# Logits and half-tile rows turned by VectorE and ScalarE instead of TensorE, with two loads and one sum moved

## The chip, the cores and the metric

The kernel runs on one core of a Trainium2 chip. The metric is the device time of one launch in microseconds (us). A profile of one execution comes with the times; in it PE is TensorE (PEld its weight loads), DVE is VectorE, ACT is ScalarE, POOL is GpSimd and SP is SyncE, and L12 is line 12 of the kernel.

## The reference

Linear attention with decay over 4 sequences of 768 tokens and 8 heads of 64, and on its output (3072 rows of 512) a mixture of 8 experts with a sticky choice of expert:

```python
for b in range(nb):                       # blocks of the sequence
    intra = einsum('bhic,bhjc->bhij', qb, kb) * Dmask
    intra = einsum('bhij,bhjd->bhid', intra, vb)
    inter = einsum('bhid,bhde->bhie', qb * lam_pow, kv_state)
    out[:, :, sl] = intra + inter
    kv_state = lam_block * kv_state + einsum('bhsd,bhse->bhde', kb_dec, vb)
...
logits = x @ w_gate;  local_gate = sigmoid(x @ w_local)
for s in range(S):                        # along each sequence
    e = argmax(logits[b, s]) if s == 0 or local_gate[b, s] < 0.5 else prev_e
    p = softmax(logits[b, s])
    out[b, s] = p[e] * (relu(x[b, s] @ w1[e]) @ w2[e])
```

w1 is 8 x 512 x 1024 and w2 is 8 x 1024 x 512. All is in fp32.

## The kernel before

**Attention half** (lines 785 to 842). 24 steps s, one for each block of 128 tokens of each of the 4 sequences, blocks outermost. A step multiplies queries and keys of a later step (`scores`, L196 to L212: on TensorE, then VectorE's product with the decay mask into `sm`), adds the state's part (`from_state`, L235) and the block's part (`mix`, L248), which ScalarE copies to `xc` (L251), brings the state up to date (`update`, L262 to L267), and turns the rows of the step before and writes them to a DRAM buffer (`rows_of`, L272 to L281). `WIDE` lists the steps whose scores are made with 128 keys in one matmul (L200); the others use two matmuls of 64 keys, the second of which leaves out queries that the mask makes zero (L208).

After every fourth step, `gates(k)` (L286) multiplies four finished blocks by the gate's weights. The 512 features lie in four groups of 128, and group d's partial logits come out on partitions 32d to 32d+8 of the bank `pl`, tokens along the free axis. ScalarE copies them to `lg` (L289). `logits(k)`, in the next step but for the last group, turns `lg` by four transposes on TensorE (L294), and VectorE adds the four partial sums of each token into `lt` (L295), which has tokens on partitions. From `lt` VectorE finds experts (`fresh_experts`, L399 to L403, its last output being `mark`), TensorE and VectorE follow them along the sequences (L411 to L420), rank the tokens, and build lists of rows for tiles of 128 tokens that share an expert. This routing is spread over the steps by the table `extras` (L771).

In this half the orders of PE, DVE, SP and POOL are those of the program text (L785). ScalarE's order is left to the scheduler of the framework, up to L916.

**First tiles** (L871 to L916). Five tiles of 128 rows go through `hidden` (L731, relu in L733) and `output` (L737), weights for each from `weights` on SP's queue. The rows are gathered by POOL's indirect DMA (L703). `flipped` (L717) turns 32x32 blocks of a gathered tile on VectorE, and `moved` (L724) brings the blocks to their places by 16 copies of 32 partitions, as a rule on ScalarE; `ks` names which quarters of the tokens it moves.

**Pairs** (L975 to L1077, from L1180 on with the orders of PE, DVE, SP and ACT by hand). Two tiles of one expert are multiplied together by a scheme with seven products for eight (`product_1` L957, `product_2` L962), which needs sums of blocks of the weights (`sums_1`, `sums_2`, L935 to L938) and of the rows (`sums_of_x`), all on VectorE. The last sum of `sums_2`, index 3, writes `s2[:, 2]`, read by the last but one product of the pair (L1064). While a pair runs, the next pair's two tiles are flipped and moved (L989, L990, L996, L1042 to L1059). Eight pairs run in the profiled execution, with three full tiles between the third and the fourth.

**Half tiles** of up to 64 rows are worked off in the first two pairs: `hook(0)` to `hook(13)` are places in a pair's program, and `hooks_of_halves` (L1128) puts a half's four steps on successive places. With three halves, as here, the first begins at hook 7 of pair 0, the second at hook 0 of pair 1 and the third at hook 7 of pair 1. The first has at most 32 rows. `turned_part` (L1083) turns the gathered rows `xgh` by four transposes on TensorE (L1086) and one copy on VectorE (L1088); `hidden_of_part` (L1096), `hidden_turned` (L1106) and `output_of_part` (L1118) follow. The halves' weights use a third pair of buffers, `w1t[2]` and `w2t[2]`.

**SP's queue** around the start of the pairs: the first layer of the first pair (L911), both layers of the first half (`weights_of(G2, 2)`, L914), then the second layer of the first pair (L1182). Each is 2 MB, and each waits until its buffer has been read for the last time: the first pair's second layer until `output(1, 1)` is done.

Of the kernel before, what the change touches and what calls it, by code (L numbers as in the profile page):

```python
# [38 lines left out]
PARTS = [(0, 8), (8, NA), (NA, NT)]  # L39
LOADS = 6  # L40
QUARTERS = [16, 17, 18, 19]
WIDE = [3, 4, 5, 6]
WARM = 10
KA = -(-(NA * P - E * (P - 1)) // P)

# [19 lines left out]
def kernel(  # L65
# [217 lines left out]
    def gates(k):  # L283

        for d in range(DT):
            nc.tensor.matmul(pl[EP * d:EP * d + EP], lhsT=wgt[:, d], rhs=xc[:, d].rearrange("p b i -> p (b i)"),  # L286
                             start=True, stop=True, skip_group_check=True)
        lg = lgs[k] = rt.tile([P, B * P], F32, name="lg")
        nc.scalar.copy(lg, pl)  # L289

    def logits(k):
        lg = lgs.pop(k)
        for j in range(B):
            nc.tensor.transpose(pl[:, P * j:P * j + P], lg[:, P * j:P * j + P], ident)  # L294
        nc.vector.tensor_reduce(lt[:, B * k:B * k + B],  # L295
                                pl.rearrange("p (j d e) -> p j e d", j=B, e=EP)[:, :, :E + 1],
                                axis=AX.X, op=ALU.add)

    pl = pg.tile([P, B * P], F32, name="pl")
    pr = pg.tile([P, DM], F32, name="pr")  # L300
# [381 lines left out]
    def weights_of(g, i, layers=(1, 2), cond=None, own=None):  # L682
        e = expert(g, own)
        if 1 in layers:
            nc.sync.dma_start(out=w1t[i], in_=w1_src(e), cond=cond, cond_hint=None if cond is None else True)
        if 2 in layers:
            nc.sync.dma_start(out=w2t[i], in_=w2_src(e), cond=cond, cond_hint=None if cond is None else True)
# [31 lines left out]
    def moved(xt, xq, ks=range(4), copy=nc.scalar.copy):  # L719

        blocks = xq.rearrange("p (d j i) -> p d j i", j=4, i=QP)
        for k in ks:
            for j in range(4):
                copy(xt[QP * j:QP * j + QP, :, QP * k:QP * k + QP], blocks[QP * k:QP * k + QP, :, j])  # L724
# [60 lines left out]
    with tc.manual_schedule(engines={PE, DVE, SP, POOL}):  # L785
# [16 lines left out]
        for s in range(NS):  # L802
            if s + LOADS - 1 < NS:
                loaded(s + LOADS - 1)
            if s + 3 < NS and s != 1:
                prepare(s + 3)
            if s in QUARTERS:
                j = QUARTERS.index(s)
                nc.sync.dma_start(out=w1t[0][:, j], in_=w1_src(0)[:, j])
            if s == NS - 4:  # L810
                nc.sync.dma_start(out=w2t[0], in_=w2_src(0))
                weights(0)
            if s == NS - 1:
                nc.sync.dma_start(out=w1t[1], in_=w1_src(1))
                nc.sync.dma_start(out=w2t[1], in_=w2_src(1))
            if s + 1 < NS and s not in (1, 2, 3, 4, 5):
                scores(s + 1)
            from_state(s)
            if s % B == 1 and s > B:
                logits(s // B - 1)  # L820
            if s == 5:
                scores(6)
            extra_work(s, 0)
            if s % B == 0 and s:
                gates(s // B - 1)
            mix(s)
            if s == 0:
                update(0)
                query_powers(0)
            if s in (1, 2, 3, 4):  # L830
                scores(s + 1)
            if s == 1:
                query_powers(1)
                prepare(4)
                rows_of(0)
            if s:
                update(s)
            if s + 1 == NS:
                first_turned()
            if s > 1:  # L840
                rows_of(s - 1)
            extra_work(s, 1)
# [38 lines left out]
        moved(xtt[1], xq, (2, 3))  # L881
        hidden(0, 0, 1)
        by_slots(0, (2, 3, 4))
        logits(NC - 1)
        fresh_experts(2)
        flipped(xqs[1], xgt[0])
        ahead(4, 0)
# [23 lines left out]
        weights_of(KA, w_of(0), (1,))  # L911
        output(1, 1, range(FT // 2))
        by_slots(1, (0, 1, 2, 3, 4))
        weights_of(G2, 2)  # L914
        output(1, 1, range(FT // 2, FT))
        written(3, 1)  # L916

# [4 lines left out]
    def xp(p, j):  # L922
        return xps[2] if j else xps[p % 2]
# [21 lines left out]
    def sums_2(p, ns):  # L945
        fs = sums(s2, b2(p, 0, 0), b2(p, 0, 1), b2(p, 1, 0), b2(p, 1, 1), False)
        for n in ns:
            fs[n]()
# [5 lines left out]
    def product_1(to, a, b, new=False):  # L954
        for m in range(FT // 2):
            for k in range(2):
                nc.tensor.matmul(to[:, m], lhsT=a[:, k, P * m:P * m + P], rhs=b[:, k], start=(new and not m and not k),  # L957
                                 stop=(k == 1), skip_group_check=True)
# [13 lines left out]
    def pair_moved(p, i):  # L972
        moved(xp(p, i), xqs[i])

    def pair(p, hooks={}, next=True, load=True, cond=None, write=True, further=True):  # L975

        def hook(k):
            for f in hooks.get(k, ()):
                f()
# [7 lines left out]
        nc.scalar.copy(c01, a)  # L987
        if next:
            pair_flipped(0)  # L989
            pair_moved(p + 1, 0)  # L990
        hook(0)
        product_1(b, s1[:, 1], xs[:, 1], True)
        tt(c10, c01, b, ALU.add)
        hook(1)
        sums_2(p, (0, 1))
        if next:  # L996
            pair_flipped(1)
# [6 lines left out]
        tt(c11, c11, c, ALU.add)  # L1004
        nc.scalar.activation(h11, c11, ACT.Relu)
        hook(3)
        sums_2(p, (2, 3))
        product_1(a, a1(p, 0, 1), b1(p, 1, 0))
        nc.scalar.activation(h00, a, ACT.Relu)
        hook(4)  # L1010
# [46 lines left out]
        hook(10)  # L1057
        if next:
            moved(xp(p + 1, 1), xqs[1], (3,))  # L1059
            sums_1(p + 1, (2, 3))  # L1060
        product_2(a, h01, b2(p, 1, 0))
        gated(c00, a, g1)
# [17 lines left out]
    def ahead_half(h):  # L1080
        collect(xgh, 1, G2 - KA + h)

    def turned_part(n):  # L1083
        pt = pg.tile([P, DT, P], F32, name="po1")
        for d in range(DT):
            nc.tensor.transpose(pt[:, d], xgh[:, P * d:P * d + P], ident)  # L1086
        xt = act.tile([P, DT, HP], F32, name="xth", bufs=1)[:, :, :P // n]
        nc.vector.tensor_copy(xt, pt[:, :, :P // n])  # L1088
        return xt

    def hidden_of_part(xt, n):
# [36 lines left out]
    def hooks_of_halves(n, first):  # L1128

        now = {}  # L1130
        hooks = {}

        def add(k, f):
            hooks.setdefault(k, []).append(f)

        def steps(h):
            cols = 2 if h else first

            def start():
                now["xt"] = turned_part(cols)  # L1140
                if h + 1 < n:
                    ahead_half(h + 1)

            def middle():
                now["hs"] = hidden_of_part(now["xt"], cols)

            def turn():
                now["ht"] = hidden_turned(now["hs"], cols)

            def end():  # L1150
                output_of_part(h, now["ht"], cols)
                if h + 1 < n:
                    weights_of(G2 + h + 1, 2)

            return start, middle, turn, end

        for h in range(n):
            place = 2 + 6 * h // n if n <= 6 else 8 - n + h
            k = (0, 3, 7, 10)[place % 4] + 14 * (place // 4)
            for j, f in enumerate(steps(h)):  # L1160
                add(k + j, f)
        return hooks

    def one_of(value, choices, label, arm):
# [15 lines left out]
    with tc.manual_schedule(engines={PE, DVE, SP, ACTE}):  # L1180
        more, fulls, halves = (number(k, n) for k, n in enumerate((PMAX - PMIN + 1, E + 1, FIRST_SMALL + 1)))
        weights_of(KA, w_of(0), (2,))  # L1182
        both_halves()
        pair_ahead(0)
        rows_out(1)
# [147 lines left out]
```

## Time and profile before

| | us |
|---|---|
| median of 3 runs | 451.74 |
| lowest, highest | 450.8, 454.43 |
| the profiled execution | 451.95 |
| its span, first to last instruction | 450.1 |
| start of the first pair's products, of the second pair's | 178.5, 211.1 |
| one steady pair (343.98 to 368.64) | 24.66 |
| end of the last pair's products | 442.6 |

The granted TensorE clock is 0.994 of full speed. A row of the groups reads: line, engine, operation, output<-inputs with their shapes, count, then busy us in total and mean ns of one, then idle us of the engine just before them. A row of a timeline reads: start and length in us, engine, line, operation, count, and in brackets the idle time before it and what ended that.

### The profile page before, as it was taken

The numbers are of one execution on the slowest core, as the hardware profiler recorded it, in microseconds if no ns is written. First come the engines' busy times: TensorE is split into PE (matmuls) and PEld (weight loads), VectorE is DVE, ScalarE is ACT, GpSimd is POOL, SyncE is SP. The second block draws the span as 40 slices with busy tenths as digits, with TensorE's granted clock in tenths as the row PEclk, the third lists the DMA queues.
The fourth block names the chain that finished last, engine by engine and source line by source line (L and its number), as shares of the span: only waits on it lengthen the run. The fifth ranks groups of instructions, "written<-read, shape, count | busy, mean of one in ns | idle before, by whom it ended". The sixth has DMA issues, their size and how long they took to land.

```text
span 450.1 us, 10497 instructions
## 1 busy us (share of the span) xinstructions
PE 431.8 (96%) x4186; PEld 358.5 (80%) x4186; DVE 278.9 (62%) x562; ACT 201.7 (45%) x594; POOL 109.3 (24%) x120
## 2 busy tenths in 40 slices
PE   6999998899999999799999999999999999999993
PEld 5877786778667776788685999677799999898982
DVE  5547776871429949576463796100487888878661
ACT  2356665547454104543524448441445455556110
POOL 4476565231100041203220400110102011020101
PEclk9999999999999999999999999999999999999997
DMA  8999999979899899999994499997163838380101
GB/s 269 409 420 411 327 305 317 360 260 367 310 375 353 287 400 379 358 387 399 388 345 176 145 404 375 352 348 286 43 211 93 309 103 284 147 280 6 52 3 51
DMA packets 42575, 124.85 MB, mean 277 GB/s; under 512 B 3148, under 2 KB 3148, under 8 KB 40592
## 3 DMA queue, kind: packets, MB, share of 16 engines
q1 hardware_dynamic: 34976, 104.62, 63.4%
q0 software_dynamic: 4368, 13.90, 9.0%
q10 hardware_dynamic: 3168, 5.51, 3.2%
q8 instruction: 37, 0.61, 0.5%
q14 instruction: 26, 0.21, 0.1%
HBM read 124.02 MB, written 12.91 MB: 304 GB/s over the span
## 4 chain that ended last, share of the span: by engine, by line
PE 77%; DMA 12%; issue 6%; DVE 4%; POOLq 0%; POOL 0%
PE ps L731 11%; PE pk L962 11%; PE pk L737 11%; PE ps L957 10%; DMA out_dram<-y,sidxp 6%; PE po L248 5%; DMA w<-in_w_dram 5%; PE po L957 5%; PE pl L962 4%; PE ps L208 3%; PE pk L272 3%; PE pk L262 2%; PE po L235 2%; PE pr L1118 2%; PE pr L1096 2%
## 5 line engine op out<-in xcount | busy, mean ns | idle before, releaser
L731 PEld LDWEIGHTS ps<-xt,w 128*128 128x128 f32 x512 | 58.2, 192 | 3.0 <-issue 2.3
L731 PE MATMUL ps<-xt,w 128*128 128x128 f32 x512 | 59.1, 276 | 0.3 <-DVE xt L713 0.3
L737 PE MATMUL pk<-w,h 128*128 128x512 f32 x128 | 56.5, 593 | 0.0
L737 PEld LDWEIGHTS pk<-w,h 128*128 128x128 f32 x128 | 23.6, 190 | 26.3 <-issue 25.6
L703 POOL DMA_INDIRECT xg<-x_dram,gidx x25 | 25.8, 1032 | 59.2 <-DVE lg L717 27.7
L746 POOL DMA_INDIRECT out_dram<-y,sidx x14 | 14.0, 1001 | 105.8 <-DVE y L763 46.5
L212 DVE TENSOR_TENSOR sm<-ps,mask 128x512 f32<-128x512 f32 x46 | 29.7, 685 | 15.1 <-PE ps L208 7.6
L724 ACT COPY xp<-xlast 32x128 f32<-32x128 f32 x128 | 37.8, 295 | 1.7
L733 ACT ACTIVATE h<-ps 128x512 f32<-128x512 f32 x16 | 9.6, 597 | 57.6 <-PE ps L731 57.6
L724 ACT COPY xp<-lg 32x128 f32<-32x128 f32 x112 | 33.0, 295 | 2.6
L763 DVE TENSOR_SCALAR y<-pk,gate 128x512 f32<-128x512 f32 x8 | 5.9, 743 | 42.1 <-PE pk L737 30.4
L957 PEld LDWEIGHTS ps<-xp,w 128*128 128x128 f32 x256 | 30.5, 192 | 1.7 <-issue 1.3
L177 POOL TENSOR_TENSOR qd<-inp,lamq 128x512 f32<-128x512 f32 x20 | 25.6, 1278 | 24.9 <-PE po L235 11.4
L957 PE MATMUL ps<-xp,w 128*128 128x128 f32 x256 | 31.3, 275 | 0.0
L957 PE MATMUL ps<-xs,s 128*128 128x128 f32 x256 | 31.2, 275 | 0.0
L962 PE MATMUL pk<-w,h 128*128 128x256 f32 x128 | 30.5, 381 | 0.0
L962 PE MATMUL pk<-s,hsum 128*128 128x256 f32 x128 | 30.3, 380 | 0.0
L248 PE MATMUL po<-sm,inp 128*64 128x128 f32 x384 | 27.7, 280 | 2.5 <-DVE sm L212 1.6
L957 PEld LDWEIGHTS ps<-xs,s 128*128 128x128 f32 x256 | 29.9, 192 | 0.0
L248 PEld LDWEIGHTS po<-sm,inp 128*64 128x64 f32 x384 | 20.9, 136 | 9.5 <-issue 6.6
L962 PEld LDWEIGHTS pk<-s,hsum 128*128 128x128 f32 x128 | 23.9, 190 | 3.3 <-DVE s L1045 0.2
L962 PEld LDWEIGHTS pk<-w,h 128*128 128x128 f32 x128 | 23.5, 190 | 3.4 <-issue 0.6
(280 smaller groups left out, 792.0 us busy)
## 6 DMA issues: line engine op xcount, KB each, us to landing
w<-in_w_dram SPq DMA_DIRECT2D x43, 2048.0 KB, 11.4
inp<-in_qkv_dram SPq DMA_DIRECT2D x15, 1024.0 KB, 8.0
x_dram<-xn ACTq DMA_DIRECT2D x21, 256.0 KB, 7.2
inp<-in_qkv_dram SPq DMA_DIRECT2D x10, 512.0 KB, 7.7
inp<-in_qkv_dram SPq DMA_DIRECT2D x4, 768.0 KB, 6.3
w<-in_w_dram SPq DMA_DIRECT2D x4, 512.0 KB, 9.8
x_dram<-xn SPq DMA_DIRECT2D x2, 256.0 KB, 8.1
xg<-x_dram,gidx POOLq DMA_INDIRECT x25, 6.8
```

The source lines that it names most:

```text
L177: nc.gpsimd.tensor_tensor(qd, x[:, 0].rearrange("p (a i) -> p a i", i=P), lamq, ALU.mult)
L208: nc.tensor.matmul(ps[u][half, a, first:], lhsT=kt[rows, a, half], rhs=qt[rows, a, first:], start=True, stop=True, skip_group_check=True)
L212: nc.vector.tensor_tensor(sm[:, u], ps[u], mask[:, u], ALU.mult)
L248: nc.tensor.matmul(head(a, u), lhsT=vn[:, a, u], rhs=sm[:, u, a], start=(not c and a < 2), stop=True, skip_group_check=True)
L272: nc.tensor.transpose(px[:, P * a:P * a + P], xc[:, a, ORDER[s][0]], ident)
L703: nc.gpsimd.indirect_dma_start(out=xg, out_offset=None, in_=x_dram[:n, :], in_offset=bass.IndirectOffsetOnAxis(ap=gidx[i][:, j:j + 1], axi ...
L724: copy(xt[QP * j:QP * j + QP, :, QP * k:QP * k + QP], blocks[QP * k:QP * k + QP, :, j])
L731: nc.tensor.matmul(ph[:, j], lhsT=w1t[w][:, d, P * f:P * f + P], rhs=xtt[i][:, d], start=(d == 0), stop=(d == DT - 1))
L737: nc.tensor.matmul(pys[i], lhsT=hq[f // 4, i][:, f % 4], rhs=w2t[w][:, f], start=(f == 0), stop=(f == FT - 1))
L746: apart(nc.gpsimd.indirect_dma_start(out=out, out_offset=bass.IndirectOffsetOnAxis(ap=sidx[i][:, j:j + 1], axis=0), in_=y, in_offset=None, ...
L957: nc.tensor.matmul(to[:, m], lhsT=a[:, k, P * m:P * m + P], rhs=b[:, k], start=(new and not m and not k), stop=(k == 1), skip_group_check= ...
L962: nc.tensor.matmul(to, lhsT=a[:, f], rhs=b[:, f], start=(new and not f), stop=(f == FT // 2 - 1), skip_group_check=True)
```

## The change

- `WIDE` keeps step 3 only.
- `gates` turns the bank `pl` into `lg` by VectorE's transpose of 32x32 blocks. `logits` copies the partial sums of groups 1 to 3 to the first 32 partitions by three copies on ScalarE, adds them to those of group 0 by three adds on VectorE, and copies the total to the four quarters of the partitions of `lt` by four copies on ScalarE. The room for it is a buffer of `hq` that is free at the time.
- The first half's weights (`weights_of(G2, 2)`) are issued after the first pair's second layer on SP's queue instead of before it.
- In a pair, the 16 moves of the next pair's first tile are issued in three parts, around `hook(0)` and after `hook(1)`, and the last sum of `sums_2` goes from after `hook(3)` to after `hook(10)`, ahead of the last two sums of `sums_1`.
- The halves' rows are turned by `flipped` on VectorE and `moved` on ScalarE. These two steps have places of their own ahead of the product, given by `sooner` in hooks: for the first and the third half, flip at hook 3 and move at hook 5 of the pair; for the second, both at hook 12 of pair 0. The gather of the next half follows the flip. The buffer `xqs[0]` is the one that a pair's first tile is flipped into.

```diff
-WIDE = [3, 4, 5, 6]
+WIDE = [3]
...
         lg = lgs[k] = rt.tile([P, B * P], F32, name="lg")
-        nc.scalar.copy(lg, pl)
-
-    def logits(k):
-        lg = lgs.pop(k)
-        for j in range(B):
-            nc.tensor.transpose(pl[:, P * j:P * j + P], lg[:, P * j:P * j + P], ident)
-        nc.vector.tensor_reduce(lt[:, B * k:B * k + B],
-                                pl.rearrange("p (j d e) -> p j e d", j=B, e=EP)[:, :, :E + 1],
-                                axis=AX.X, op=ALU.add)
+        nc.vector.transpose(lg, pl)
+
+    def logits(k, room):
+        n = B * P // EP
+        lg = lgs.pop(k).rearrange("p (n e) -> p n e", e=EP)[:, :, :E + 1]
+        parts = room.rearrange("p f i -> p (f i)")[:EP, :(DT - 1) * n * (E + 1)]
+        parts = parts.rearrange("p (d n e) -> p d n e", d=DT - 1, e=E + 1)
+        for d in range(1, DT):
+            nc.scalar.copy(parts[:, d - 1], lg[EP * d:EP * d + EP])
+        for d in range(1, DT):
+            nc.vector.tensor_tensor(parts[:, 0], lg[:EP] if d == 1 else parts[:, d - 1], parts[:, 0], ALU.add)
+        total = parts[:, 0].rearrange("p (b j) e -> p b j e", b=B)
+        for j in range(P // EP):
+            nc.scalar.copy(lt[EP * j:EP * j + EP, B * k:B * k + B], total[:, :, j])
...
             if s % B == 1 and s > B:
-                logits(s // B - 1)
+                logits(s // B - 1, hq[1, 0])
...
-        logits(NC - 1)
+        logits(NC - 1, hq[0, 1])
...
         by_slots(1, (0, 1, 2, 3, 4))
-        weights_of(G2, 2)
         output(1, 1, range(FT // 2, FT))
...
         if next:
             pair_flipped(0)
-            pair_moved(p + 1, 0)
+            moved(xp(p + 1, 0), xqs[0], (0,))
         hook(0)
+        if next:
+            moved(xp(p + 1, 0), xqs[0], (1,))
         product_1(b, s1[:, 1], xs[:, 1], True)
         tt(c10, c01, b, ALU.add)
         hook(1)
+        if next:
+            moved(xp(p + 1, 0), xqs[0], (2, 3))
         sums_2(p, (0, 1))
...
         hook(3)
-        sums_2(p, (2, 3))
+        sums_2(p, (2,))
...
             moved(xp(p + 1, 1), xqs[1], (3,))
+        sums_2(p, (3,))
+        if next:
             sums_1(p + 1, (2, 3))
         product_2(a, h01, b2(p, 1, 0))
...
-    def turned_part(n):
-        pt = pg.tile([P, DT, P], F32, name="po1")
-        for d in range(DT):
-            nc.tensor.transpose(pt[:, d], xgh[:, P * d:P * d + P], ident)
+    def moved_part(n):
         xt = act.tile([P, DT, HP], F32, name="xth", bufs=1)[:, :, :P // n]
-        nc.vector.tensor_copy(xt, pt[:, :, :P // n])
+        moved(xt, xqs[0], range(4 // n))
         return xt
...
-            def start():
-                now["xt"] = turned_part(cols)
+            def flip():
+                flipped(xqs[0], xgh)
                 if h + 1 < n:
                     ahead_half(h + 1)
+
+            def move():
+                now["xt"] = moved_part(cols)
...
-            return start, middle, turn, end
+            return flip, move, middle, turn, end
...
-            for j, f in enumerate(steps(h)):
-                add(k + j, f)
+            sooner = {0: (2, 2), 3: (1, 0), 7: (4, 2), 10: (3, 2)}[k % 14]
+            for j, f in zip((-sooner[0], -sooner[1], 1, 2, 3), steps(h)):
+                if k + j < 0:
+                    f()
+                else:
+                    add(k + j, f)
...
         weights_of(KA, w_of(0), (2,))
+        weights_of(G2, 2)
         both_halves()
```

## The prediction

> **What bounds the kernel now.** I read the page's busy shares first, then its 40 slices, then the groups by form, then timelines of three places.
>
> ```profile
> PE 431.8 (96%) x4186; PEld 358.5 (80%) x4186; DVE 278.9 (62%) x562; ACT 201.7 (45%) x594; POOL 109.3 (24%) x120
> PE   6999998899999999799999999999999999999993
> ...
> DMA  8999999979899899999994499997163838380101
> ```
>
> TensorE (PE) is at work in nearly every slice, so its time is what the kernel takes: an instruction taken off it is worth its own time, and a new wait on it costs its own length. DMA is close to full until slice 17 (some 190 us), so there the order of transfers counts.
>
> ```profile
> L294 PE MATMUL pl<-ident,lg 128*128 128x128 f32 x24 | 3.9, 286 | 0.0
> L200 PE MATMUL ps<-inp 64*128 64x128 f32 x64 | 4.6, 285 | 0.0
> L1086 PE MATMUL po<-ident,xgh 128*128 128x128 f32 x12 | 1.8, 272 | 0.0
> L717 DVE STREAM_TRANSPOSE lg<-xg 128x512 f32<-128x512 f32 x11 | 7.7, 700 | 0.0
> L724 ACT COPY xp<-xlast 32x128 f32<-32x128 f32 x128 | 37.8, 295 | 1.7
> ```
>
> These groups (busy us and mean ns of one after the bar) are what leaves TensorE and what takes its place. Matmuls overlap, so a mean of 286 ns isn't the price: the next group starts 0.58 us after the first of four L294 (60.05 to 60.63 us in the timeline) and 0.43 us after four L1086 (212.90 to 213.33).
>
> The one long stop of TensorE after 103 us is in the first pair:
>
> ```profile
> 161.77 6.79 SPq L687 DMA_DIRECT2D w<-in_w_dram  x2
> ...
> 186.09 1.22 DVE L937 TENSOR_TENSOR s<-w 128x1024 f32<-128x1024 f32 x1 [2.97 <-DMA w<-in_w_dram]
> ...
> 189.81 0.69 DVE L1004 TENSOR_TENSOR part<-part,po 128x512 f32<-128x512 f32 x1
> 190.54 2.05 PE L957 MATMUL po<-xs,w 128*128 128x128 f32 x16 [2.95 <-DVE part L1004]
> ```
>
> VectorE, which keeps program order, stands at the second-layer sums (L937) until weights land at 186.0; L1003 and L1004 are queued behind them, and the product that reuses L1004's bank waits 2.95 us (brackets: idle time before, and who ended it). The chain of waits has the load from 164.55 to 186.09.
>
> A steady pair has no gap on TensorE (24.66 busy of 24.66 us from 343.98), but little room at its end:
>
> ```profile
> 363.66 0.48 DVE L1055 SCALAR_TENSOR_TENSOR y<-pk,gate,rest 128x256 f32<-128x256 f32 x1 [0.36 <-PE pk L962]
> 364.18 0.48 DVE L1056 SCALAR_TENSOR_TENSOR y<-pl,gate,y 128x256 f32<-128x256 f32 x1
> 364.58 1.21 DVE L936 TENSOR_TENSOR s<-s,w 128x1024 f32<-128x1024 f32 x1
> ...
> 365.18 1.89 PE L962 MATMUL pl<-s,h 128*128 128x256 f32 x8
> ```
>
> The matmul of 365.18 is the product with s2[:, 2], the sum that the change puts at the place of the L936 of 364.58.
>
> [...] each L717 is followed by 32-partition copies that move the blocks. [...] the load issued at 164.55 took 21.5 us behind three others. [...] Here the narrow scores with 32 matmuls take 0.72 us to the next group (31.04 to 31.76), the wide with 16 take 1.09 (19.48 to 20.57).
>
> **The change part by part**, against the profiled execution (451.95 us, span 450.1 and 1.85 around it; 0.2 above the median of the three runs).
>
> 1. Logits off TensorE. Five groups of L294 at 0.58 and the last at 0.47 (111.98 to 112.45): **-3.4**. In their place, for each group: VectorE gains a transpose (0.70; reading PSUM isn't shown, so 0.70 to 0.80) and three adds of 144 columns [...] and loses the reduce (0.30): +1.3 us. ScalarE loses a copy of 0.58 and gains three of 144 columns [...] and four of 36 [...]: +1.2 us. Both have idle time, but the logits now take two crossings. In step 9 of the attention loop, before:
>
> ```profile
> 44.75 0.30 DVE L295 TENSOR_REDUCE lt<-pl 128x36 f32<-128x144 f32 x1
> ...
> 46.10 0.17 DVE L403 SCALAR_TENSOR_TENSOR mark<-lt,best 128x8 bf16<-128x8 f32 x1
> ...
> 47.77 0.27 PE L411 MATMUL pr<-identb,mark 128*4 128x128 bf16 x2
> ```
>
> Now VectorE does the adds 44.85 to 45.8, ScalarE the four copies to 46.6, and L399 to L403 (1.3 us) end near 47.9. L411, 0.58 earlier, wants mark at 47.2: a wait of 0.7, and about the same in step 14. VectorE is also full from 89.7 to 99.8 us, with some 0.8 us idle; one transpose and one set of adds (+1.3) put the scores' mask product of step 23 (98.55 before, wanted by TensorE at 100.33, now 99.75) about 0.9 late. Sum 2.3; the idle 0.8 gives back some, so I take **+2.0**. Lower end 0 (ScalarE's order in this half is chosen by the scheduler, and mask products are made a step ahead); upper end in rival B. Behind the waiting VectorE stand the state add L265 and the next mask products; behind ScalarE's copies the xc copies, which free the bank for the next step's L235.
>
> The last group (logits of step 23) has slack: fresh_experts starts some 1.6 us later than 113.06, its mark (114.39 before) is wanted at 119.41. Nothing; without that cover 1.6.
>
> 2. WIDE. Scores of steps 4, 5 and 6: three times 1.09 less 0.72 to 0.83 (the latter 12.51 to 13.34): **-1.0** (0.8 to 1.1). TensorE has no gap there. Inputs are fetched five steps ahead, so the fuller DMA of 10 to 42 us (about 415 GB/s) doesn't show at once.
>
> 3. Weights. The second-layer load can't leave sooner: it still waits for output(1, 1), done at 164.4. But two loads of 2 MB (first half tile) no longer stand ahead of it; at 400 GB/s each is 5.2 us, so it lands about 173 to 176, ahead of 183.1, where its sum is first wanted. Then L1004 ends as in a steady pair (product 2.02 after its predecessor there): near 187.7 instead of 190.5. **-2.85** (0 if it lands after 186). On SP's queue the half tile's two loads now wait behind that wait; they land near 187, wanted at 198.2 less 3. Nothing; the cover is some 8 us. Pair 1's loads, issued at 183.8, land up to 2 us later (about 193 and 198); sums_1 wants the first at 195.9.
>
> 4. Half tiles. Three L1086 groups at 0.43: **-1.3**. VectorE: three flips of 0.70 for copies of 0.29, 0.42, 0.42; ScalarE: 4+8+8 copies of 0.295 = 5.9 us. The gather of the next half on POOL (1.0) follows the flip instead of the transposes. The first and third half are moved at hook 5, over 1 us before their product: nothing. The second is flipped at hook 12, after sums_of_x: in the old times VectorE ends sums_2(3) and both L936 near 210.0, L1065 and sums_of_x 212.2, the flip 212.9; eight copies to 215.4; TensorE wants them at 214.7. **+0.7** (0 to 1.5). The next pair's flip waits for the same buffer, and its L993 behind it (216.2), which nobody on TensorE misses before 218.8.
>
> 5. sums_2(3) to hook 10. It can't start before L1056: product b ends at 363.46, L1055 and L1056 take it to 364.6, the sum to 365.8, while the product that reads it was due at 365.18. Wait 0.65 in each of the five pairs that go on without a half tile at hook 10 (2 to 6), 0.7 in the last (L1056 438.16, product 439.17), 0.1 in pairs 0 and 1, where a half's 64 or 32 matmuls give cover: **+4.15** (3.5 to 5). Earlier in the pair VectorE has 1.2 us more room, which TensorE didn't lack.
>
> 6. Moves of a pair's first tile in three parts: the same 16 copies, wanted only at the pair's end; ScalarE is busy 13.4 of 24.66 us. Nothing (4.7 per pair without that cover).
>
> Sum: -3.4 -1.0 -2.85 -1.3 +2.0 +0.7 +4.15 = **-1.7**, so 450.25 in the profiled execution, **450.0** as a median.
>
> **The rivals.** A: the sum of part 5 costs nothing, because TensorE reaches that product late for other reasons: 451.95 - 5.85 - 0.2 = 445.9. For it: five other parts move in a pair; against it: the 1.72 us between the products and the 2.3 us of VectorE stand in every steady pair. B, the other side: ScalarE's in-order queue in the attention half becomes the bound. An Exp (L477) waited 3.06 and 2.15 us there for VectorE, with the logits' and xc copies behind it; the mean 2.6 less 1.2 us of slack between xc copies and L235 (46.0 to 47.23) makes 1.4, times five, 7.0 more: 457.0. The kernel is slower than before from 3.8 us of waits there, 0.76 per group. Against it: the four copies come at most 1 us after VectorE's adds. C: the weights' gain doesn't come (landing after 186, or pair 1's loads late by as much): 452.9.
>
> **How the numbers follow.** My forecast 0.48, A 0.25, B 0.16, C 0.11. Within 1% (447.2 to 456.3; about what a measurement of this kernel can tell from no change) lie the forecast (0.45 of its 0.48; 0.02 faster, 0.01 slower), all but 0.01 of C, which is slower, and 0.02 of B; A is faster but for 0.01. So faster 0.26, same 0.58, slower 0.16. The range holds most of A and ends short of B: 445.5 to 455.5. The forecast's own range is 447.5 to 453.
>
> **What would show it.** No L294 and L1086; the load landing before 176 and L1004 without a wait in pair 0; a gap of 0.65 ahead of the s2[:, 2] product in each steady pair (pairs of 25.3 instead of 24.66 us); L411 waiting for mark. I am wrong if the pairs stay at 24.66, if ScalarE's copies hold up L235, or if a half tile waits for its weights.

## The result, and the profile after

The kernel after takes 458.98 us (median of 5 runs, 455.56 to 459.79) where the kernel before takes 452.8 beside it: a ratio of 1.0145, interval 1.010 to 1.0189. A second set of six runs, on the chip on which half of the experiments ran, gave 458.85 and 1.0154 (1.0112 to 1.0196). The profiled execution was the fastest of its set: 455.56 us, span 453.8, at a granted clock of 0.996; the other four had 0.989 to 0.991. So its trace shows 3.6 us of the loss, and the rest goes with the clock, to which a section below returns.

| us | before | after |
|---|---|---|
| first tile's products start | 102.79 | 105.46 |
| first pair's products start | 178.50 | 181.05 |
| second pair's | 211.11 | 210.18 |
| a steady pair | 24.66 | 25.43 |

So the attention half loses 2.7 us, the first pair wins 3.5, and each pair loses 0.77. The busy row of the page comes first:

```profile
PE 430.3 (95%) x4198; PEld 355.1 (78%) x4198; DVE 287.2 (63%) x580; ACT 214.5 (47%) x650; POOL 109.9 (24%) x120
```

TensorE is busy for 1.5 us less and the span is 3.7 us longer: what left it did not pay for the new waits. The list of TensorE's waits in the attention half (10 to 103 us: who waited for whom, total, times, longest), after:

```profile
PE pr L416 <- DVE mark L408: 4.5, 2, 2.3
PE po L248 <- DVE sm L212: 1.4, 1, 1.4
PE pk L262 <- DVE kv L265: 1.2, 1, 1.2
PE po L235 <- issue: 1.0, 1, 1.0
```

Before, the whole list was 1.4 + 1.2 + 0.9 + 0.2 us of "issue" (no engine was waited for) and 0.5 us of VectorE. After, TensorE waits for VectorE there in place after place, 8.2 us in all. The timeline of step 9 shows why mark (L403 before, L408 now) is late:

```profile
43.54 1.29 DVE L212 TENSOR_TENSOR sm<-ps,mask 128x512 f32<-128x512 f32 x2
...
44.11 1.28 POOL L177 TENSOR_TENSOR qd<-inp,lamq 128x512 f32<-128x512 f32 x1 [0.85 <-PE po L235]
44.75 0.80 DVE L299 TENSOR_TENSOR h<-lg,h 32x144 f32<-32x144 f32 x1
...
45.56 1.05 POOL L180 TENSOR_TENSOR kd<-inp,rev 128x512 f32<-128x512 f32 x1 [0.17 <-PE pk L262]
45.66 1.51 DVE L299 TENSOR_TENSOR h<-h 32x144 f32<-32x144 f32 x2
...
47.20 0.91 ACT L302 COPY lt<-h 32x36 f32<-32x36 f32 x4 [1.78 <-DVE lt L394]
...
49.34 0.17 DVE L408 SCALAR_TENSOR_TENSOR mark<-lt,best 128x8 bf16<-128x8 f32 x1
...
49.57 0.27 PE L416 MATMUL pr<-identb,mark 128*4 128x128 bf16 x2 [2.31 <-DVE mark L408]
```

The three adds took 2.31 us, not the 0.95 of the prediction (44.85 to 45.8). The merged row of 1.51 us is two of them, 1.11 and 0.30. Each of the first two ends 0.16 us after a GpSimd (POOL) multiply that began before it; the third, with GpSimd idle, took 0.30.

In the first pair the step that the prediction was surest of came as told. L1004 is now L1012, and the product behind it L961; the same view, after:

```profile
185.59 1.21 DVE L941 TENSOR_TENSOR s<-w 128x1024 f32<-128x1024 f32 x1
...
189.28 0.69 DVE L1012 TENSOR_TENSOR part<-part,po 128x512 f32<-128x512 f32 x1
...
190.03 2.05 PE L961 MATMUL po<-xs,w 128*128 128x128 f32 x16
```

There is no bracket on L941 and none on the product: the weights were there, and neither VectorE nor TensorE waited. And the end of a steady pair, after (the chain of waits passes through this sum):

```profile
363.96 0.48 DVE L1063 SCALAR_TENSOR_TENSOR y<-pk,gate,rest 128x256 f32<-128x256 f32 x1 [0.52 <-PE pk L966]
364.48 0.48 DVE L1064 SCALAR_TENSOR_TENSOR y<-pl,gate,y 128x256 f32<-128x256 f32 x1
364.88 1.22 DVE L942 TENSOR_TENSOR s<-w,s 128x1024 f32<-128x1024 f32 x1
...
366.15 1.99 PE L966 MATMUL pl<-s,h 128*128 128x256 f32 x8 [0.50 <-DVE s L942]
```

The product of s2[:, 2] waits for its sum (L942), 0.50 us in every pair that has no half tile there, and runs 1.99 instead of 1.89 us.

### The profile page after: what moved, and what is told of

Its sections match the earlier page's. It is cut to its first block, busy times and chain, and to the rows that moved or that the text cites. A ratio compares the mean times of both kernels' runs of the same rounds, so it can differ in the third digit from the quotient of the medians.

```text
span 453.8 us, 10595 instructions
## 1 busy us (share of the span) xinstructions
PE 430.3 (95%) x4198; PEld 355.1 (78%) x4198; DVE 287.2 (63%) x580; ACT 214.5 (47%) x650; POOL 109.9 (24%) x120
## 4 chain that ended last, share of the span: by engine, by line
PE 37%; DMA 6%; issue 5%; DVE 3%; ACT 0%; POOLq 0%; POOL 0%; ACTq 0%
PE ps L961 9%; PE pk L966 8%; DMA out_dram<-y,sidxp 6%; PE ps L736 5%; PE pk L742 5%; PE po L961 4%; PE pl L966 4%; PE pr L1125 2%; PE pr L1103 2%; DVE s L942 1%; DVE s L940 1%; ACT xth L729 0%; DVE y L1063 0%; DVE y L1064 0%; POOLq L1344 0%
## 5 line engine op out<-in xcount | busy, mean ns | idle before, releaser
L742 PEld LDWEIGHTS pk<-w,h 128*128 128x128 f32 x128 | 23.6, 190 | 26.3 <-issue 25.8
L961 PEld LDWEIGHTS ps<-xp,w 128*128 128x128 f32 x256 | 30.4, 192 | 2.2 <-issue 1.9
L961 PE MATMUL ps<-xp,w 128*128 128x128 f32 x256 | 31.4, 276 | 0.2 <-PE pk L966 0.2
L961 PE MATMUL ps<-xs,s 128*128 128x128 f32 x256 | 31.2, 275 | 0.0
L961 PEld LDWEIGHTS ps<-xs,s 128*128 128x128 f32 x256 | 29.9, 192 | 0.0
L180 POOL TENSOR_TENSOR kd<-inp,rev 128x512 f32<-128x512 f32 x20 | 22.2, 1112 | 19.2 <-DMA inp<-in_qkv_dram 9.7
```

Of the source, the lines that this page charges most:

```text
L180: nc.gpsimd.tensor_tensor(kd.rearrange("p (h d) -> p h d", d=DH), x[:, 3].rearrange("p (h d) -> p h d", d=DH), rev.unsqueeze(2).broadcast_ ...
L742: nc.tensor.matmul(pys[i], lhsT=hq[f // 4, i][:, f % 4], rhs=w2t[w][:, f], start=(f == 0), stop=(f == FT - 1))
```

## The experiments

All are of the whole kernel, beside runs of the kernel before on the same chip; ratios are to those runs. Each starts from the kernel before or after, as said.

**The sum back** (from after):

```diff
-        sums_2(p, (2,))
+        sums_2(p, (2, 3))
...
-        sums_2(p, (3,))
```

> The changed kernel with the last sum of sums_2 back after hook 3. Theory (that sum is late for the last but one product in every pair): steady pairs go from 25.43 to 24.66 us, the last pair loses its 0.50 us wait; about 4.5 us less than the changed kernel, so 454.5 as a median, 1.004 of before. Rival (the place after hook 3 is worse now, because the half tile's flip stands there too): pairs 0 and 1 grow by 0.3 to 0.7 us each before the second product of the second layer, and 3.5 us or less are won.

Measured: 453.68 us, 1.0013 (0.9991 to 1.0035), steady pairs of 24.66 to 24.71 us again. So the sum costs 5.2 us in this kernel. The traces show 4.8 of it, from the start of the first pair's products to the end of the last pair's (265.5 us in the kernel after, 260.7 here).

**The logits back on TensorE** (from after: `gates`, `logits` and their calls as before).

> The changed kernel with the logits turned by TensorE again; all else stays changed. Theory (the logits' way over ScalarE and VectorE makes mark and a few mask products late, some 8 us of TensorE waits against 3.4 us of transposes saved): TensorE reaches the first tile's products near 101.3 us instead of 105.5, the waits of 2.3 and 2.2 us for mark are gone, and the time falls by about 4.2 us to 454.8. Rival (the attention half lost its time to the narrow scores of steps 4 to 6 or to inputs that come late): the first tile starts at 103 us or later, and 2 us or less are won.

Measured: 455.48 us, 1.0070 (1.0046 to 1.0094). TensorE has the six groups of transposes again, and the kernel is 3.4 us faster for it. But the first tile starts at 104.46 us, not near 101.3: TensorE has 4.8 us of stops for nothing visible in this half, so the rival holds in part.

**Both back** (what is left of the change: load order, half tiles, narrow scores, moves in parts).

> Logits and the sum both as before; what stays of the change is WIDE, the order of the loads, the moves in three parts and the half tiles off TensorE. Theory: the two costs add up, so 8.7 us less than the changed kernel, and faster than before by the gains of the other parts: WIDE 1.0 to 1.4, loads 2.85, half tiles 0.6, so 448 as a median, 0.990 of before. Rival (the gains are an effect of the profiled execution alone, or the slower medians come from a lower granted clock that the narrow scores or the fuller engines bring about): the same as before, 452 to 453, with the clock at 0.989.

Measured: 450.76 us, 0.9955 (0.9933 to 0.9977): faster than both kernels, but by less than expected. The two costs add up: 2.9 us for the logits with the sum in its old place (453.68 less 450.76), 4.7 for the sum with the old logits.

**Adds with one input in PSUM** (from after). ScalarE copies the partial logits into the bank `pl`, which is free by then, so that no add reads two operands in SBUF:

```diff
-        parts = room.rearrange("p f i -> p (f i)")[:EP, :(DT - 1) * n * (E + 1)]
-        parts = parts.rearrange("p (d n e) -> p d n e", d=DT - 1, e=E + 1)
+        parts = pl[:EP, :(DT - 1) * n * (E + 1)].rearrange("p (d n e) -> p d n e", d=DT - 1, e=E + 1)
+        run = room.rearrange("p f i -> p (f i)")[:EP, :n * (E + 1)].rearrange("p (n e) -> p n e", e=E + 1)
...
-            nc.vector.tensor_tensor(parts[:, 0], lg[:EP] if d == 1 else parts[:, d - 1], parts[:, 0], ALU.add)
+            nc.vector.tensor_tensor(run, parts[:, d - 1], lg[:EP] if d == 1 else run, ALU.add)
```

> The changed kernel, but the three copies of partial logits go to the bank pl, so that each add reads one input from PSUM and one from SBUF. Theory (an add of two SBUF inputs stands still while a GpSimd operation runs: 0.80, and 1.51 for two, beside GpSimd's multiplications, but 0.70 for two and 0.29 for one without them): the adds take 0.3 to 0.45 us each also beside GpSimd, the two waits for mark shrink from 2.3 and 2.2 us to about 1.0, and 2 to 3 us are won against the changed kernel. Rival (adds on 32 partitions after a write of the same tile are slow of themselves): they stay at 0.75 us each, and nothing is won.

Measured: 456.42 us, 1.0092 (1.0067 to 1.0117): 2.4 us won, and the adds as short as expected, but the waits for mark stay longer than the 1.0 that was expected. The timeline of the same step in this kernel:

```profile
44.59 1.28 POOL L177 TENSOR_TENSOR qd<-inp,lamq 128x512 f32<-128x512 f32 x1 [0.85 <-PE po L235]
45.23 0.28 DVE L299 TENSOR_TENSOR h<-pl,lg 32x144 f32<-32x144 f32 x1
45.55 0.63 DVE L299 TENSOR_TENSOR h<-pl,h 32x144 f32<-32x144 f32 x2
...
47.93 1.26 POOL L177 TENSOR_TENSOR qd<-inp,lamq 128x512 f32<-128x512 f32 x1 [0.85 <-POOL kd L180]
48.18 1.04 DVE L408 SCALAR_TENSOR_TENSOR mark<-lt,best 128x8 bf16<-128x8 f32 x1
```

The same adds beside the same GpSimd multiply take 0.28 to 0.30 us each. Coming sooner, the last step (L408), whose two inputs are in SBUF, now falls beside the next multiply: 1.04 us for 8 columns that took 0.17. TensorE's wait for mark is 1.53 here instead of 2.31. (At the second mark, at 66 us, L406 is caught in the same way, 1.19 us instead of 0.19, and the wait is 1.98 instead of 2.20.) It adds up from the prediction's 0.7: plus 0.87 for L408 is 1.57; in the kernel after, plus 1.38 for the adds and 0.18 for L405 is 2.26.

**The same, and the product of mark asked for later** (sum in its old place; the second number of a key of `extras` is 0 for the middle of a step, 1 for its end):

```diff
-        (6, 1): constants_2, (7, 1): constants_3, (8, 1): constants_4, (9, 1): constants_5, (10, 1): constants_6,
-        (9, 0): lambda: fresh_experts(0), (10, 0): lambda: along_sequences(0), (11, 0): lambda: experts_of(0),
-        (12, 0): lambda: ranks(0), (13, 0): lambda: fresh_experts(1), (14, 0): lambda: (along_sequences(1), masks(0)),
+        (6, 1): constants_2, (7, 1): constants_3, (8, 1): constants_4, (9, 1): constants_5, (10, 1): lambda: (constants_6(), along_sequences(0)),
+        (9, 0): lambda: fresh_experts(0), (11, 0): lambda: experts_of(0),
+        (12, 0): lambda: ranks(0), (13, 0): lambda: fresh_experts(1), (14, 0): lambda: masks(0), (14, 1): lambda: along_sequences(1),
...
```

> The kernel after with the sum of s2[:, 3] back at its old place (453.68 us by itself), and two edits to the logits: the partial logits are copied into PSUM, so that no add of VectorE has both its inputs in SBUF, and the product that reads mark is asked for at the end of its step instead of at its beginning. If what the logits cost was their lateness for that product (waits of 2.31 and 2.20 us there), these waits are gone, the first tile's products start near 102.5 us instead of 106.68, and the time is 449.5 to 450. Rival: VectorE itself is too full in the attention half, and what isn't waited for at the mark is waited for at the masks' products (sm) and at the state (kv) of the following steps: 452.5 or more, with the waits on sm and kv over 2 us longer in sum.

Measured: 453.3 us, 1.0002 (0.9983 to 1.0021). The rival's time and waits came. The longest waits of TensorE in this kernel:

```profile
PE pk L262 <- DVE kv L265: 2.3, 2, 1.4
PE po L248 <- DVE sm L212: 2.1, 4, 1.2
PE pr L432 <- DVE run L425: 2.1, 2, 1.4
```

Against the kernel with only the sum back (453.68) the two edits won 0.4 us, which is within the noise. No wait for mark is left, and as much has come up at the state (kv), at the masks' products (sm) and at `run`, the next result of the routing. But VectorE isn't too full in those steps, as the rival had it. The timeline of step 9 in this kernel:

```profile
45.83 0.91 ACT L302 COPY lt<-h 32x36 f32<-32x36 f32 x4 [0.31 <-DVE lt L394]
...
46.78 0.22 DVE L404 TENSOR_REDUCE mx<-lt 128x8 f32<-128x64 f32 x1 [0.97 <-ACT lt L302]
...
47.56 1.27 POOL L177 TENSOR_TENSOR qd<-inp,lamq 128x512 f32<-128x512 f32 x1 [0.85 <-POOL kd L180]
...
47.80 1.05 DVE L408 SCALAR_TENSOR_TENSOR mark<-lt,best 128x8 bf16<-128x8 f32 x1
...
48.78 0.41 DVE L265 TENSOR_TENSOR kv<-pk,kv 128x256 f32<-128x256 f32 x1
...
49.34 0.69 PE L262 MATMUL pk<-inp,kd 128*64 128x64 f32 x16 [0.95 <-DVE kv L265]
```

VectorE stands 0.97 us for ScalarE's four copies, with the state's sum (L265) behind it in program order, and then L408 still falls beside GpSimd's multiply. At the second mark it stands 1.41 us, and L406 takes 1.22. So the edits moved the wait to the next thing in VectorE's order and left its causes. This is read from the trace; no run takes these causes away.

**The load order alone** (from before):

```diff
-        weights_of(G2, 2)
         output(1, 1, range(FT // 2, FT))
...
         weights_of(KA, w_of(0), (2,))
+        weights_of(G2, 2)
```

> The kernel before, with only the first pair's second-layer load put ahead of the first half tile's loads. If the prediction's part 3 holds as it stood, the 2.97 us that VectorE stood for these weights and TensorE's 2.95 us wait behind L1004 are gone, and 2.85 us with them: 450.2 us where the kernel before has 453.06 (ratio 0.994). Rival: the later loads of pair 1, pushed back by the same 2 MB, make a new wait in pair 1 and take most of it back: 452.5 or more.

Measured: 448.87 us, 0.9907 (0.9878 to 0.9935). In its trace the first pair takes 29.54 us instead of 32.61 (start of its products to start of the second pair's), 3.07 less, and the second has no new wait. The median won 1.3 us more than that; the granted clocks of the runs point to where: their median is 0.996, the kernel before's 0.991. Of the 39 runs of the kernel before beside it, the 14 with a clock of 0.994 or more have a median of 452.0, and the load order, whose runs all have that clock, is 3.1 below: at one clock the gain is the trace's.

**The half tiles alone** (from before, with the moves in three parts):

> The kernel before, with only the half tiles' rows turned by VectorE and ScalarE (and the moves of a pair's first tile in three parts, which share their buffer). Part 4 says 1.3 us less on TensorE and 0.7 more at the second half: 452.45 (ratio 0.9987). Rival: the second half's late moves cost more than the three groups of transposes gave, 453.5 or more, with a wait of over 1.3 us ahead of L1097.

Measured: 456.2 us, 1.0079 (1.0044 to 1.0115): a loss, as the rival had it, but the rival's wait ahead of L1097 isn't in the trace. The first two pairs are 0.23 and 0.69 us shorter, so the half tiles win what they should. The loss is in the last pair, where they have no part. Its timeline:

```profile
416.35 0.38 PE L957 MATMUL ps<-xp,w 128*128 128x128 f32 x2
419.04 2.75 PE L957 MATMUL ps<-xp,w 128*128 128x128 f32 x14 [2.31 <-issue]
421.57 2.71 PE L957 MATMUL ps<-xs,s 128*128 128x128 f32 x16
```

Two of 16 matmuls, a stop of 2.31 us that nothing visible ends, and then matmuls at two thirds of their pace (the granted clock is 0.50 from 420 to 422 us and 0.81 from 422 to 425). One thing moves just then. The DMA view of 416.5 to 417.0 us, same kernel:

```profile
q8 instruction: 1, 0.02, 13.4%
```

(queue, packets, MB, share.) The packet starts at 416.60, and the stop ends 2.44 us later. In the attention half of the kernel before, packets of this queue start 4 to 8 us apart, with some 244 of TensorE's instructions (matmuls and weight loads) from one to the next, and each of the five stops for nothing visible ends 2.3 to 2.4 us after one: packets start at 35.01, 47.10, 70.07, 82.99 and 89.70, and stops end at 37.39, 49.47, 72.39, 85.39 and 92.00. The longest of them:

```profile
72.39 0.44 PE L235 MATMUL po<-qd,kv 64*64 64x128 f32 x4 [1.41 <-issue]
```

**The same, 18 instructions of TensorE fewer at the start** (`WARM` is the number of warm-up matmuls):

```diff
-WARM = 10
+WARM = 1
```

> The kernel with the half tiles alone (456.2 us), with one instead of ten warm-up matmuls at its very start, so that everything TensorE reads later stands 18 instructions nearer to the start of its program. Theory: the stop of 2.31 us in the last pair is TensorE waiting for its own next instructions, and where in the program it falls is an accident of the count: 9 matmuls of 0.13 us later there it shrinks or goes, and the time falls by 1.5 to 2.3 us, to 454 to 454.7. Rival: the stop belongs to the half tiles or to the last pair's data, and stays at 416.7 us with 2 of 16 matmuls done: 456 or more.

Measured: 452.4 us, 0.9993 (0.9969 to 1.0017). That product is unbroken now:

```profile
418.32 1.95 PE L957 MATMUL ps<-xp,w 128*128 128x128 f32 x16
```

A stop of 0.29 us is left in the next product, and it too ends 2.46 us after a packet. The last pair takes 25.28 us instead of 29.03. The two traces differ elsewhere (the first tile starts 0.8 us sooner, and the first pair is 3.0 us longer, at half clock after its wait), so it is the last pair's length, more than the medians, that places the 3.8 us. The length of that stop went with how many of TensorE's instructions stand ahead of it in the program: 18 fewer, and 2.31 us became 0.29. That TensorE waits there for its own next instructions is the author's reading. The traces show the packets and the stops that end 2.3 to 2.5 us after one, not what TensorE waits for.

**The narrow scores alone** (from before):

```diff
-WIDE = [3, 4, 5, 6]
+WIDE = [3]
```

> The kernel before, with only the scores of steps 4, 5 and 6 in narrow tiles. Part 2 of the prediction says 1.0 us less, kept to the end: 452.05 (ratio 0.998), and the first tile's products near 101.8 us instead of 102.79. Rival, suggested by the run with both undone, which reached that point at 103.66 although its steps 4 to 6 were as short: the lead is lost again before step 23 to stops on TensorE that no engine's result ends, so nothing or up to 1 us slower: 453.0 to 454.

Measured: 456.38 us, 1.0071 (1.0042 to 1.0100): the rival's side, and beyond it. TensorE reaches the first tile at 105.82 instead of 102.79, with 5.5 us of stops for nothing visible instead of 3.8; after the longest of them (1.99 us, to 85.11) the granted clock is 0.50 from 86 to 88 us. In this execution the first pair loses 2.0 us more: its wait (3.35 us) is followed by half clock, 0.51 from 195 to 197 us; in the profile of the kernel before the clock stays at 1.00 there.

**Load order, with two steps more in wide tiles** (steps 14 and 15), and **with eight more** (8, 10, 12, 14, 15, 16, 18, 20): the other direction.

> The kernel with the load order alone (448.87 us), with the scores of steps 14 and 15 in wide tiles too: 2 x 0.37 us more work on TensorE, 64 instructions fewer. Theory: in the attention half TensorE is short of instructions[...], so that narrow tiles only trade work for stops: the stops of 0.75 us at 67 and 1.90 us at 73.8 shrink by 1 us or more together, and the time is 448.2 to 448.9. Rival: the stops have nothing to do with the count of instructions and stay: 449.6.

> The load order alone (448.87 us), with wide scores in eight more steps (8, 10, 12, 14, 15, 16, 18 and 20): 8 x 0.37 = 3.0 us more work on TensorE and 256 instructions fewer. With two more wide steps the stops before 103 us had already shrunk from 3.7 to 1.1 us. If shortage of instructions was the cause, there is little left to win and the rest is work: 2.2 us more than with two steps, less at most 1.1: 449.6 to 450.7. If wide tiles were better for another reason (each winning over 0.5 us), it goes on falling: 446 or less.

Measured: 448.47 us, 0.9912 (0.9882 to 0.9941), and 448.68, 0.9912 (0.9893 to 0.9931). With two, the stops fall from 3.7 us (load order alone) to 1.1 and the first tile starts at 100.09 instead of 103.77; with eight, stops of 1.0 us and 102.75. So more work with fewer instructions cost no time that shows, which speaks for the shortage of instructions that the expectations suppose, but eight wide steps should by the expectation have cost at least 1 us more than they did: the size isn't settled.

**The kernel after, with wide scores:**

> The kernel after with the scores of steps 4, 5 and 6 in wide tiles again, and nothing else. If the narrow scores are a loss by themselves because TensorE runs short of instructions, 2.5 to 3 us are won: 455.9 instead of 458.85. If part 2 of the prediction holds inside this kernel, it is 1.0 us slower: 459.9. A stop of 2.3 to 2.6 us in the last pair, as in the runs with the half tiles and wide scores, would take the win back: then 458.4, with that stop in the trace.

Measured: 460.33 us, 1.0173 (1.0147 to 1.0199). By the ratios that is 0.9 us slower than the kernel after (1.0154), within the noise of the two, and nearest to part 2 of the prediction (1.0). The traces agree: the first tile starts at 109.04 us instead of 107.94 (second profile of the kernel after, below). Further on this trace has a half tile that waits 1.2 us for its weights, and a last pair of 26.44 us instead of 25.58 with a stop of 0.57 us. So the narrow scores don't cost anything in this kernel. Alone they cost 3 us; why not here, beside the waits for VectorE, was not shown.

**Load order and half tiles**, with the old wide scores and with steps 14 and 15 added:

> The kernel before, with the load order and the half tiles off TensorE, without the narrow scores. By itself the load order made 448.87, and with the half tiles and the narrow scores it was 450.76. If the narrow scores are what costs there, 448.0 (the half tiles then win the 0.6 to 0.9 us that pairs 0 and 1 show); if the half tiles cost, as they did alone, 451 or more, with a new stop on TensorE in the last pair or elsewhere.

> Load order, half tiles off TensorE and the scores of steps 14 and 15 in wide tiles too (64 instructions fewer than in the run with load order and half tiles, whose last pair had a stop of 2.57 us). If that stop moves out of the last pair, 447.7 (448.47 less the 0.7 us of the half tiles); if it stays, 450.5.

Measured: 451.64 us, 0.9977 (0.9953 to 1.0000), and 447.64, 0.9902 (0.9869 to 0.9934). The second has no stop in the last pair; the first has one of 2.57 us, again after two matmuls, in its timeline:

```profile
412.05 0.39 PE L956 MATMUL ps<-xp,w 128*128 128x128 f32 x2
415.00 1.83 PE L956 MATMUL ps<-xp,w 128*128 128x128 f32 x14 [2.57 <-issue]
```

The version with steps 14 and 15 has the lowest median of all, though the load order alone (0.9907) can't be told from it. The first can hardly be told from the kernel before; the second beats both kernels.

**The kernel after, again:**

> The kernel after, unchanged, beside the others on the same chip. By the sum of the parts undone (2.9 for the logits, 4.7 for the sum, 2.3 won by the rest, on 453.06) it should be at 458.4; if its first five runs were low in clock by accident, at the 455.6 us of its profiled execution.

Measured: 458.85 us, so the first five runs were no accident. This time the profiled execution was a usual one, 457.88 us at a clock of 0.989. The windows of its TensorE (stretch, length, busy us, count, granted clock, DMA share, GB/s), and those of the execution profiled first:

```profile
49.00:53.00 4.00, 3.85 (x42) 0.58 0.46 170
...
105.00:109.00 4.00, 3.98 (x27) 0.66 1.02 403
```

```profile
49.00:53.00 4.00, 3.43 (x86) 1.00 0.71 238
...
105.00:109.00 4.00, 3.65 (x33) 1.00 1.02 408
```

The first window follows the same wait for mark of 2.31 us in both. In one execution TensorE went on at full clock, in the other at about half for some 3 us: 42 matmuls of the window against 86. The second follows the wait of 1.43 us for the mask product of step 23. At like clocks (0.9895 and less) the four such runs of this set have a median of 459.0 and the seven of the kernel before 454.8, so 4 us of the loss stand at one clock, and the rest is that the kernel after runs at the lower clock more often (a median of 0.989 in its six runs, of 0.991 in the kernel before's).

## Why the prediction was wrong

It said 450.0 us, -1.7 from its profiled execution; the median is 6 us above the kernel before and outside the range. The step that failed most is the logits (item 1); the half tiles and the sum cost more than was said too. Going from before to after one edit at a time, by the ratios above times 453 us (each step to 1.5 or 2 us, and in this order; another order would share the sum out differently):

| step | predicted | measured | from |
|---|---|---|---|
| load order | -2.85 | -4.2 | 0.9907 |
| half tiles, moves in parts | -0.6 | +3.2 | 0.9977 after 0.9907 |
| narrow scores | -1.0 | -1.0 | 0.9955 after 0.9977 |
| logits | -1.4 | +2.6 | 1.0013 after 0.9955 |
| sum | +4.15 | +6.4 | 1.0154 after 1.0013 |
| sum of all | -1.7 | +7.0 | |

1. **Logits: the step that failed most.** Its term was "three adds of 144 columns", 0.95 us by an estimate of the author's that no trace showed, and, built on it, waits of "+2.0" against 3.4 us taken off. The adds took 2.31 us in step 9, and the waits for VectorE in the attention half are 8.2 us instead of 0.5. The estimate was near for an add with VectorE alone (0.30) and wrong beside GpSimd's multiplies (0.80 and 1.11), two of which stand in the timeline of before just where the adds were to go, from 44.85 to 45.8 (the second comes 0.58 us sooner once the transposes are gone):

```profile
44.11 1.28 POOL L177 TENSOR_TENSOR qd<-inp,lamq 128x512 f32<-128x512 f32 x1 [0.85 <-PE po L235]
...
46.15 1.04 POOL L180 TENSOR_TENSOR kd<-inp,rev 128x512 f32<-128x512 f32 x1 [0.76 <-PE pk L262]
```

The first wait, 0.7, was right without them; mark is 4.5 of the 8.2 us, and 1.4 were said. The next two parts, the state (1.2) and the mask product of step 23 (1.4, where 0.9 was said), show in the kernel after as:

```profile
81.74 1.28 POOL L177 TENSOR_TENSOR qd<-inp,lamq 128x512 f32<-128x512 f32 x1 [2.06 <-PE po L235]
81.81 1.22 DVE L524 TENSOR_TENSOR taken<-ends,table 128x8 f32<-128x8 f32 x1
...
99.61 0.19 DVE L483 TENSOR_REDUCE kd<-kd 128x4 f32<-128x32 f32 x1 [1.13 <-ACT kd L482]
```

L524 is an operation of the routing on 8 columns, both inputs in SBUF, that took 0.17 us before; here it fell beside a multiply, with the state's sum behind it. At step 23 it isn't, as the prediction had it, that VectorE is full: it stands 1.13 us (0.29 before) for an Exp that ScalarE takes after the four copies into `lt`. So the adds are only part of it: with one input in PSUM the kernel after won 2.4 us (458.85 to 456.42), but with the sum in its old place the same edit and a later asker together won 0.4. The rest is the two crossings, at which VectorE itself stands still with other work in its order behind, and what else they push beside GpSimd. That split is read from the traces, not shown by a run.

2. **Narrow scores.** The work was priced rightly. Two of the kernels above differ by nothing else (load order and half tiles, and "both back"): in the traces the rows of block 5 are turned at 33.03 us and 32.24, so most of the 1.0 is there. Then it is lost to stops, and the first tile starts at 100.61 and 103.66. That the number in the chain agrees is luck: there the extra 96 instructions also took the stop out of the last pair (27.66 us and 24.83). Alone they cost 3 us; in the kernel after, nothing. "TensorE has no gap there" was true of the trace before, but its stops for nothing visible later in that half, 3.8 us, were in the same trace and went unread. What they cost in a given kernel stays open.

3. **Load order.** Mechanism and place right. The term of 2.85 us was 3.07 in the trace and 4.2 in the median: the rest goes with the clock, a median of 0.996 in the runs without this wait and of 0.991 in the kernel before's.

4. **Half tiles.** Right in size where they run (0.9 us won in two pairs). What isn't in the sum at all is the stop in the last pair, which takes 29.03 us instead of 24.83 with the half tiles alone. In the kernel after there is no such stop; adding the narrow scores had taken it away, as item 2 says.

5. **Sum.** The mechanism, the place and nearly the size: the product starts 0.67 us later in a steady pair, where 0.65 was said, and itself takes 0.10 more. That makes 0.77 us a pair, 4.6 in six pairs, where 4.15 was said. The 4.7 us found with the old logits are this. In the kernel after it is 5.2 to 6.4, part of which can be the lower clock there (median 0.989 against 0.9935 with the sum back).

6. **Moves in parts.** Nothing, as said, as far as the traces show: no pair has a wait for them. No run has them alone.

Rival B had the side (slower, 457.0), but its mechanism, ScalarE's queue holding up the xc copies, is not what the trace shows: the late engine is VectorE, and ScalarE's order shows in the Exp of step 23 only. A and C fell: the sum does cost, and the loads did win.

## What to carry to other kernels

Before work is moved to an engine, look at what the neighbouring engines run at that very moment, and at where the operands lie: a duration from a quiet place does not hold beside GpSimd (here 0.80 and 1.11 us for an add of two inputs in SBUF, instead of 0.30). Ask also what stands behind the new work in its engine's order: here 3.4 us off TensorE, busy 96% of the time, were worth less than the waits of 8.2 us that new crossings between two other engines brought. And when an edit changes the time in a place that it doesn't touch, look at the stops that no engine ends before explaining it: here a shift of 18 instructions was worth 3.8 us in the last pair, against 0.9 that the half tiles won where they run.

## What the runs showed of the hardware

- VectorE instructions with both inputs in SBUF, beside a GpSimd multiply that began before them, ended 0.01 to 0.16 us after it: 0.80 and 1.11 us instead of 0.30 for 144 columns, 1.04 and 1.22 instead of 0.17 for 8. With one input in PSUM the 144 columns took 0.28 to 0.30 beside the same multiply.
- VectorE's transpose of 128x512 out of PSUM took 0.71 us, as long as from SBUF (0.70).
- TensorE stopped up to 2.6 us with no releaser; in the kernel before each of five such stops ended 2.3 to 2.4 us after a packet of the instruction queue started. A shift by 18 instructions cut one such stop from 2.31 to 0.29 us and the last pair by 3.8 us.
- A stop of TensorE was sometimes paid twice. After the first pair's wait of 3.4 us in the run with the half tiles and one warm-up matmul, the windows of that kernel show half the clock for over 6 us:

```profile
189.00:192.00 3.00, 2.71 (x12) 0.50 0.98 344
192.00:195.00 3.00, 3.00 (x16) 0.50 1.05 398
195.00:198.00 3.00, 3.00 (x18) 0.99 1.04 397
```

  From 186 to 189 us the clock is 0.87; worked out from these four windows, the low stretch is some 6.8 us at half clock. Two others come to some 3.4 in the same way: with the narrow scores alone 0.96, 0.50 and 0.69 over the three stretches of 2 us from 84, and after the wait for mark in the second profile of the kernel after 0.58 over 49 to 53 and 0.99 over the next 4. One and the same stop costs clock in some executions only: behind that wait of 2.31 us the clock is 0.58 in one execution and 1.00 in the other. Its length alone doesn't decide it: half the clock followed stops of 2.31 us (the wait for mark, and the last pair with the half tiles alone), 1.99 (the narrow scores alone) and 1.43 (the mask product of step 23), while after one of 2.57 us TensorE went on at full pace (14 matmuls in 1.83 us).
